# A one-element load moved from the scalar queue into the sync queue, behind the first large load

**Chip, cores, metric.** One NeuronCore of a Trainium2 chip. The metric is the device time of one execution, in microseconds (us).

## The reference

```python
def reference(x, fx, alpha):        # x, fx: bf16 [512, 32, 640]; alpha: bf16 [1]
    return x + alpha * fx
```

x, fx and the result are 20.97 MB each, so 62.92 MB have to move, and VectorE does one multiply-add per element.

## The kernel before

Over 128 partitions each tensor is 128 x 81920, cut into five units of U = 16384 columns (4.19 MB). Every large transfer is issued by the sync engine, in program order. The only other transfer is alpha's one element, issued by the scalar engine (ACT); TensorE spreads it over 128 lanes by a matmul with ones, and VectorE copies it out of PSUM as `a_f`, which all six multiply-adds read.

```python
def alpha_to_lanes(nc, consts, psum, alpha, eng):
    a_1 = consts.tile([1, 1], alpha.dtype, name="a_1")
    eng.dma_start(out=a_1[:], in_=alpha[None, :])
    ones = ...                                      # memset to 1.0 on VectorE
    nc.tensor.matmul(a_ps[:], ones[:], a_1[:], start=True, stop=True)
    nc.vector.tensor_copy(out=a_f[:], in_=a_ps[:])
    return a_f
# ... (cut)
    a_f = alpha_to_lanes(nc, consts, psum, alpha, nc.scalar)
    t_0 = wide.tile([P, 2 * U], x.dtype, tag="a", name="t_0")
    nc.sync.dma_start(out=t_0[:, :U], in_=xv[:, :U])       # x
    nc.sync.dma_start(out=t_0[:, U:], in_=fxv[:, :U])      # fx
# ... (cut)
    x_12 = load_pair("b", 1)                               # 8.4 MB
    f_1 = load_f(1)
    add(t_0[:, :U], t_0[:, U:])
    store(0, t_0[:, :U])
    f_2 = load_f(2)
# ... (cut: x_34 into t_0's buffer, f_3, f_4, the other adds and stores)
```

Of the kernel before, what the change touches and what calls it, by code (L numbers as in the profile page):

```python
# [1 line left out]

# [4 lines left out]

ACT = mybir.ActivationFunctionType
ALU = mybir.AluOpType
F32 = mybir.dt.float32  # L10
BF16 = mybir.dt.bfloat16

U = 16384


def alpha_to_lanes(nc, consts, psum, alpha, eng):

    P = nc.NUM_PARTITIONS
    a_1 = consts.tile([1, 1], alpha.dtype, name="a_1")
    eng.dma_start(out=a_1[:], in_=alpha[None, :])  # L20
    ones = consts.tile([1, P], alpha.dtype, name="ones")
    nc.vector.memset(ones[:], 1.0)  # L22
    a_ps = psum.tile([P, 1], F32, name="a_ps")
    nc.tensor.matmul(a_ps[:], ones[:], a_1[:], start=True, stop=True)  # L24
    a_f = consts.tile([P, 1], F32, name="a_f")
    nc.vector.tensor_copy(out=a_f[:], in_=a_ps[:])  # L26
    return a_f


@with_exitstack  # L30
def kernel(
    ctx: ExitStack,
    tc: tile.TileContext,
    x: bass.AP,
    fx: bass.AP,
    alpha: bass.AP,
    out: bass.AP,
):
    nc = tc.nc
    P = nc.NUM_PARTITIONS  # L40
    xv = x.flatten_outer_dims().rearrange("(p n) d -> p (n d)", p=P)
    fxv = fx.flatten_outer_dims().rearrange("(p n) d -> p (n d)", p=P)
    ov = out.flatten_outer_dims().rearrange("(p n) d -> p (n d)", p=P)
    F = xv.shape[1]
    assert F == 5 * U

    consts = ctx.enter_context(tc.tile_pool(name="consts", bufs=1))
    psum = ctx.enter_context(tc.tile_pool(name="psum", bufs=1, space=bass.MemoryType.PSUM))
    wide = ctx.enter_context(tc.tile_pool(name="wide", bufs=1))
    fs = ctx.enter_context(tc.tile_pool(name="fs", bufs=2))  # L50
    ctx.enter_context(tc.manual_schedule())

    a_f = alpha_to_lanes(nc, consts, psum, alpha, nc.scalar)



    t_0 = wide.tile([P, 2 * U], x.dtype, tag="a", name="t_0")
    nc.sync.dma_start(out=t_0[:, :U], in_=xv[:, :U])  # L58
    nc.sync.dma_start(out=t_0[:, U:], in_=fxv[:, :U])

    def load_pair(tag, u):
        t = wide.tile([P, 2 * U], x.dtype, tag=tag, name="x_t")
        nc.sync.dma_start(out=t[:], in_=xv[:, u * U : (u + 2) * U])
        return t

    def load_f(u):
        t = fs.tile([P, U], fx.dtype, tag="f", name="f_t")
        nc.sync.dma_start(out=t[:], in_=fxv[:, u * U : (u + 1) * U])
        return t

    def add(x_ap, f_ap):
        nc.vector.scalar_tensor_tensor(  # L72
            out=x_ap, in0=f_ap, scalar=a_f[:], in1=x_ap, op0=ALU.mult, op1=ALU.add
        )

    def store(lo, x_ap):
        nc.sync.dma_start(out=ov[:, lo : lo + x_ap.shape[1]], in_=x_ap)

    x_12 = load_pair("b", 1)
# [4 lines that stand above are left out]
    add(x_12[:, :U], f_1[:])  # L84
    x_34 = load_pair("a", 3)
    f_3 = load_f(3)
    add(x_12[:, U:], f_2[:])
    f_4 = load_f(4)
    store(U, x_12[:])
    add(x_34[:, :U], f_3[:])  # L90
    store(3 * U, x_34[:, :U])
    H = U // 2
    for j in range(2):
        add(x_34[:, U + j * H : U + (j + 1) * H], f_4[:, bass.ts(j, H)])
        store(4 * U + j * H, x_34[:, U + j * H : U + (j + 1) * H])


# [1 line left out]
_INS = ['x', 'fx', 'alpha']  # L99
_OUTS = [((512, 32, 640), 'bfloat16')]  # L100


# [23 lines left out]
```

## Time and profile before

| | before |
|---|---|
| time, median of 3 | 152.6 us (152.52 to 152.8) |
| span in the profile | 150.9 us |
| VectorE busy | 86.8 us (58%) |
| packets of the sync queue | 97.8% of sixteen engines' span |
| a_f ready / first add starts | 2.27 / 22.88 us |

The lines, and what they say of the bound, are in the prediction below.

Some words first. An engine *issues* a transfer when it puts it into its queue; the sixteen DMA engines then move it as *packets*, here one for each of 128 rows and, on each engine used, a small one at the end, the *count*, which reports on a semaphore that this engine's share has arrived. A transfer has *landed* when its last count has. The packets that a queue has waiting on one DMA engine are its *ring* there. "Packet records" and "records of landings" are the single packets and semaphore counts of the packed trace, finer than the views shown here.

### The profile page before, as it was taken

The page shows a single profiled execution, that of the slowest core. Times are in us where ns is not written, and L with a number is a line of the kernel's source. Part 1 is how long each engine was busy: PE and PEld are TensorE (multiplying, and loading weights), DVE is VectorE, ACT ScalarE, POOL GpSimd, SP SyncE. Part 2 cuts the span into 40 slices and gives each one's busy share as a digit, 9 for nine tenths or more (in the row PEclk, how much of TensorE's full clock was granted, in tenths as well). Part 3 has the DMA queues.
Part 4 walks back from the last instruction along what each step waited for, and adds up shares of the span by engine and source line. Part 5 has one row for each costly group of instructions (what it writes and reads, how often), then busy time and mean ns, then how long its engine had stood idle before and what let it go on. Part 6 is the DMA issues. An engine that isn't in the chain of part 4 may idle for free.

```text
span 150.9 us, 78 instructions
## 1 busy us (share of the span) xinstructions
PE 0.2 (0%) x1; PEld 0.1 (0%) x1; DVE 86.8 (58%) x8; POOL 0.2 (0%) x4
## 2 busy tenths in 40 slices
PE   0000000000000000000000000000000000000000
PEld 0000000000000000000000000000000000000000
DVE  0000009999600089996799980009999999991000
POOL 0000000000000000000000000000000000000000
DMA  6999996999999899999896969999996969898994
GB/s 226 417 452 426 426 556 278 556 434 400 400 426 426 278 417 417 434 478 512 382 538 295 556 278 426 478 434 426 434 565 295 556 278 556 365 426 373 447 434 178
DMA packets 1874, 62.92 MB, mean 417 GB/s; under 512 B 210, under 2 KB 210, under 8 KB 210
## 3 DMA queue, kind: packets, MB, share of 16 engines
q1 hardware_dynamic: 1872, 62.92, 97.8%
q10 hardware_dynamic: 2, 0.00, 0.0%
HBM read 41.94 MB, written 20.97 MB: 417 GB/s over the span
## 4 chain that ended last, share of the span: by engine, by line
DVE 40%; DMA 35%; another core or an unknown queue 9%; DVEq 6%; SPq 0%; issue 0%
DVE x_t L72 29%; DMA f_t<-in_fx_dram 21%; DMA t<-in_fx_dram 14%; DVE t L72 11%; DVEq L121 6%; SPq L58 0%; DVEq L72 0%
## 5 line engine op out<-in xcount | busy, mean ns | idle before, releaser
L72 DVE SCALAR_TENSOR_TENSOR x_t<-f_t,a_f,x_t 128x16384 bf16<-128x16384 bf16 (+1 forms) x5 | 69.2, 13868 | 26.9 <-DMA f_t<-in_fx_dram 26.9
L72 DVE SCALAR_TENSOR_TENSOR t<-t,a_f 128x16384 bf16<-128x16384 bf16 x1 | 17.3, 17284 | 20.6 <-DMA t<-in_fx_dram 20.6
L26 DVE COPY a_f<-a_ps 128x1 f32<-128x1 f32 x1 | 0.2, 157 | 1.1 <-PE a_ps L24 1.1
L22 DVE MEMSET ones<- 1x128 bf16 x1 | 0.2, 165 | 0.8 <-PEq L110 0.8
L24 PE MATMUL a_ps<-a,ones 1*128 1x1 bf16 x1 | 0.2, 159 | 1.9 <-DMA a<-in_alpha_dram 1.9
L110 POOL MEMSET const-bfloat16-1.0<- 128x1 bf16 x1 | 0.1, 102 | 0.0
L110 POOL MEMSET const-uint8-127<- 128x1 uint8 x1 | 0.1, 102 | 0.0
L24 PEld LDWEIGHTS <-ones 1*128 1x128 bf16 x1 | 0.1, 101 | 1.0 <-DVE ones L22 1.0
L110 POOL MEMSET const-float32-0.0<- 128x1 f32 x1 | 0.1, 99 | 0.2 <-issue 0.2
L110 POOL MEMSET const-float32-1.0<- 128x1 f32 x1 | 0.1, 99 | 0.0
## 6 DMA issues: line engine op xcount, KB each, us to landing
f_t<-in_fx_dram SPq DMA_DIRECT2D x4, 4096.0 KB, 31.9
t<-in_x_dram SPq DMA_DIRECT2D x1, 4096.0 KB, 12.3
t<-in_fx_dram SPq DMA_DIRECT2D x1, 4096.0 KB, 21.6
out_dram<-t SPq DMA_DIRECT2D x1, 4096.0 KB, 22.7
out_dram<-x_t SPq DMA_DIRECT2D x1, 4096.0 KB, 21.3
out_dram<-x_t SPq DMA_DIRECT2D x2, 2048.0 KB, 15.6
x_t<-in_x_dram SPq DMA_DIRECT2D x2, 34.7
a<-in_alpha_dram ACTq DMA_DIRECT2D x1, 0.0 KB
```

Of the source, the lines that this page charges most:

```text
L22: nc.vector.memset(ones[:], 1.0)
L24: nc.tensor.matmul(a_ps[:], ones[:], a_1[:], start=True, stop=True)
L26: nc.vector.tensor_copy(out=a_f[:], in_=a_ps[:])
L72: nc.vector.scalar_tensor_tensor(out=x_ap, in0=f_ap, scalar=a_f[:], in1=x_ap, op0=ALU.mult, op1=ALU.add)
L110: nc = _bacc.Bacc("TRN2", target_bir_lowering=False, num_devices=1)
L121: with _tile.TileContext(nc) as tc:
```

## The change

Its intent: have one issuing engine for all transfers. The element goes into the sync engine's queue behind the first x load, since nobody needs it until the first fx load has landed too.

```diff
-    a_f = alpha_to_lanes(nc, consts, psum, alpha, nc.scalar)
     t_0 = wide.tile([P, 2 * U], x.dtype, tag="a", name="t_0")
     nc.sync.dma_start(out=t_0[:, :U], in_=xv[:, :U])
+    a_f = alpha_to_lanes(nc, consts, psum, alpha, nc.sync)
     nc.sync.dma_start(out=t_0[:, U:], in_=fxv[:, :U])
```

## The prediction

> **What bounds the kernel now.** I read the page first for what is busy, then the sizes and landings of the transfers, then the start of the timeline, then the waits, and the chain of waits last. The page says that nothing but the DMA is near full:
>
> ```profile
> span 150.9 us, 78 instructions
> PE 0.2 (0%) x1; PEld 0.1 (0%) x1; DVE 86.8 (58%) x8; POOL 0.2 (0%) x4
> DMA  6999996999999899999896969999996969898994
> DMA packets 1874, 62.92 MB, mean 417 GB/s; under 512 B 210, under 2 KB 210, under 8 KB 210
> q1 hardware_dynamic: 1872, 62.92, 97.8%
> q10 hardware_dynamic: 2, 0.00, 0.0%
> ```
>
> VectorE works for 58% of the span. The DMA engines are busy in every slice, and the packets of the sync queue, q1, fill 97.8% of sixteen engines' span. The scattered 6s I read as bookkeeping, not gaps: in the page's GB/s row the slices at 278 or 295 stand beside ones at 556 or 565, over the mean, as if rows that cross a slice's edge were counted in the next. Only the first and the last slice, 226 and 178 GB/s, have no such neighbour. The scalar queue, q10, carried two packets: the one element of alpha and the count that reports it.
>
> How fast the engines can go follows from two landings (columns: issues, KB each, us from issue to landing):
>
> ```profile
> t<-in_x_dram SPq DMA_DIRECT2D x1, 4096.0 KB, 12.3
> t<-in_fx_dram SPq DMA_DIRECT2D x1, 4096.0 KB, 21.6
> ```
>
> With issue times 0.73 and 1.17 us from the timeline below, they landed at 13.0 and 22.8 us, 9.7 us apart for 4.194 MB. That is 432 GB/s. All 62.92 MB at this rate take 145.6 us. The span of 150.9 leaves 5.3 us for the way to the first packet, the slow first packets, the last landing and the drain. So this is a transfer floor with little above it, and a change moves the time only if it moves the first packet, makes an engine run out of queued packets, or adds work to the engines.
>
> The start, which is all the change touches (start, duration, engine, line, operation; in brackets the idle time before it and what ended it):
>
> ```profile
> 0.73 0.49 ACTq L20 DMA_DIRECT2D a<-in_alpha_dram  x1
> 0.73 0.38 SPq L58 DMA_DIRECT2D t<-in_x_dram  x1
> 1.17 0.43 SPq L59 DMA_DIRECT2D t<-in_fx_dram  x1
> 1.64 0.42 SPq L63 DMA_DIRECT2D x_t<-in_x_dram  x1
> 1.91 0.16 PE L24 MATMUL a_ps<-a,ones 1*128 1x1 bf16 x1 [1.91 <-DMA a<-in_alpha_dram]
> 2.11 0.52 SPq L68 DMA_DIRECT2D f_t<-in_fx_dram  x1
> 2.11 0.16 DVE L26 COPY a_f<-a_ps 128x1 f32<-128x1 f32 x1 [1.13 <-PE a_ps L24]
> 22.88 17.28 DVE L72 SCALAR_TENSOR_TENSOR t<-t,a_f 128x16384 bf16<-128x16384 bf16 x1 [20.61 <-DMA t<-in_fx_dram]
> ```
>
> The 128-lane alpha, a_f, is ready at 2.11 + 0.16 = 2.27 us, and its first user starts at 22.88, held by the first fx load. Alpha has 20.6 us to spare. The sync engine has issued its four loads by 2.63 us, and then (waits of the sync queue: us in total, times, longest):
>
> ```profile
> SPq L77 <- DVE t L72: 37.5, 1, 37.5
> ```
>
> it stands for 37.5 us until the first add is done. Two loads at the rate above are on chip when that add begins, and 12.6 MB more are queued behind them.
>
> The chain of waits puts 40% on VectorE. I don't take this as the bound: the chain follows semaphores and can't see that while an add holds it, the rings behind are full.
>
> **What the Trainium skill says.** (1) "DMA: Bandwidth & Descriptors", section "Issuing engines are not separate DMA queues": transfers started by different engines run on the same 16 DMA engines and interleave; several issuers save only the sequencer's issue time. The trace agrees on the size of that: 0.49 us on the scalar queue, 0.38 to 0.52 on the sync queue. (2) The same page, "Why a DMA increments its semaphore by 16 and not by 1": a [1,1] transfer from this kind of queue uses one engine, and a 128-partition one all sixteen. The packet counts agree: 2 on q10 (data and count), and on q1 13 transfers x (128 rows + 16 counts) = 1872. (3) The same page, "Queues, rings and completion order": on one engine, descriptors of a ring are consumed in ring order. No run here yet has a small transfer behind a large one; the change is that test. (4) "Perfetto Trace Analysis", section "Roofline": a lone core may exceed its memory share and is held by its 16 DMA engines, about 435 GB/s in total. The measured 432 agrees.
>
> **The change part by part.**
> Removed: the scalar queue's issue, 0.49 us from 0.73. It ran beside the sync engine's own issue and ended nothing on the path: 0.
> Added to the sync engine: one issue between x and fx. I take the alpha issue's own 0.49 us, plus the 0.05 us between issues (0.73 + 0.38 = 1.11, next at 1.17): fx is issued at about 1.17 + 0.54 = 1.7 us, the pair of x at 2.2, f_1 at 2.65. The engines have x to work on until about 12.3 us (the trace's records of landings show the 16 engines finishing x from 12.3 to 13.06). Slack 10.6 us, used 0.54: 0. The sync engine's next wait shrinks from 37.5 to about 37.0: it absorbs the half microsecond.
> Moved: alpha's landing. On its engine it stands behind 8 rows of x (128 rows over 16 engines), so it lands when that engine is through with x: 12.3 to 13.1 us instead of before 1.91. The matmul then starts at about 12.7, and from its start to the end of the copy took 2.27 - 1.91 = 0.36 us: a_f is ready at 12.7 to 13.5. The first add can't start before 22.8. Slack falls from 20.6 to between 9.4 and 10.2 us; cost 0.
> Engine work: the same two tiny packets, on the sync ring instead of the scalar one. The packet records give them 7 and 9 ns. A turn-around gap around them is possible, but the 16 counts at the end of each load are such packets too and leave none: 8 rows of 32 KB with a recorded median of 1.213 us make 9.70 us, which is just the distance of the two landings. I put 0.00 to 0.05 us on one engine.
> First packet: x stays the sync engine's first issue, at 0.73: 0.
> Sum: 0.0 to +0.05 us, against a scatter of the runs before of 0.28 us (152.52 to 152.8).
>
> **Rivals.**
> Alpha becomes the wait: if it were not served in ring order but after all four queued loads, it would land near 53 us (f_1's add began at 53.2). The first add would end near 71, with the engines dry from 53 on: about +17 us, 170. Ring order is against it; even a landing 9 us later than I say would still cost nothing. 1% or less.
> The issue delay carries through: all later loads 0.54 us late gives 153.1. Against it: the engines are backlogged at every one of those issues, and the 37.5 us wait absorbs the delay. 5%.
> A gap on alpha's engine: a 2-byte read from memory takes, issue to matmul, 1.91 - 0.73 = 1.2 us. If the ring stood still for all of it, every load that waits for its slowest engine is up to 1.2 us later: 153.8, still under 1%. Against: the counts leave no gap, and the engines finish a load 0.75 us apart, so part of a gap on an early engine is hidden. 7%.
> A faster start: with the scalar queue silent at 0.73, x's rows may start sooner. They start about 1.0 us after the issue, and alpha's packets went out just before them; I could see 0.1 to 0.2 us, 152.4. 10%.
>
> **Range and chances.** No term reaches 1%, and the only rival that passes 2% needs alpha over 9 us late. The middle is the time before, 152.6. For the range I take the scatter of about 0.3 us either way and stretch it a little upward for the gap and the issue delay: 152.2 to 153.1. Faster by over 2% would have to come from under 149.5 us, and there is no such slack in a span with a 145.6 us floor and an unchanged start: 0.01. Slower: 0.01. Same: 0.98.
>
> **What would show it right or wrong.** The profile after should have no q10 and 1874 packets on q1; an alpha issue of 0.4 to 0.5 us on the sync engine near 1.16 and fx's issue near 1.7; the matmul waiting for alpha until 12.3 to 13.1 us; VectorE's wait split in two, some 12 us for the matmul and 9 to 10 us for fx; the first add still at 22.9 within 0.2; the share of the sync queue within half a point of 97.8%. I am wrong if the first add starts with the copy of a_f, if a slice after the first shows a gap that a neighbour doesn't make up, or if x lands more than half a microsecond away from 13.0.

## The result, and the profile after

| | before | after |
|---|---|---|
| time, median of 6 | 152.69 us (152.38 to 152.89) | 152.5 us (152.36 to 152.73) |
| ratio, 95% interval | | 0.9992 (0.9977 to 1.0006) |
| span in the profile | 150.9 us | 150.7 us |

A ratio here is the mean time of one kernel's fast runs over that of the other's of the same rounds, so not quite the ratio of the medians quoted. This one is the same time: the interval holds 1. (The line numbers of the changed kernel are one or two lower than before.)

The page of the changed kernel: span, the DMA row of the 40 slices, and the only data queue that is left (packets, MB, share of 16 engines).

```profile
span 150.7 us, 78 instructions
...
DMA  6999996979899899999896969999996969798994
...
q1 hardware_dynamic: 1874, 62.92, 97.9%
```

q10 is gone, and its two packets are now on q1. The share is 97.9% where it was 97.8%.

The start of the changed kernel's timeline:

```profile
0.73 0.38 SPq L56 DMA_DIRECT2D t<-in_x_dram  x1
...
1.17 0.32 SPq L20 DMA_DIRECT2D a<-in_alpha_dram  x1
1.54 0.35 SPq L58 DMA_DIRECT2D t<-in_fx_dram  x1
1.94 0.54 SPq L62 DMA_DIRECT2D x_t<-in_x_dram  x1
2.52 0.51 SPq L67 DMA_DIRECT2D f_t<-in_fx_dram  x1
12.91 0.16 PE L24 MATMUL a_ps<-a,ones 1*128 1x1 bf16 x1 [12.91 <-DMA a<-in_alpha_dram]
13.11 0.16 DVE L26 COPY a_f<-a_ps 128x1 f32<-128x1 f32 x1 [12.13 <-PE a_ps L24]
22.70 17.29 DVE L71 SCALAR_TENSOR_TENSOR t<-t,a_f 128x16384 bf16<-128x16384 bf16 x1 [9.43 <-DMA t<-in_fx_dram]
```

All later issues slid by 0.3 to 0.4 us, alpha came 11 us later (matmul at 12.91 instead of 1.91), and the first add still starts when fx lands: 22.70 where it was 22.88. VectorE's one wait of 20.6 us has become two, 12.1 and 9.4. The sync engine paid for its extra issue out of the long wait that follows (waits of the sync queue):

```profile
SPq L76 <- DVE t L71: 37.0, 1, 37.0
```

37.0 us instead of 37.5, the predicted half microsecond; but only 0.4 of it is the extra issue (the last load's issue ends at 3.03 us instead of 2.63). The rest is chance: the first add ended 0.18 us earlier.

One view misleads here. The chain of waits of the changed kernel now lists alpha's issue (start, us, what):

```profile
1.17 0.32 SPq L20
1.49 0.06 issue
1.54 21.03 DMA t<-in_fx_dram
```

It looks like 0.38 us more on the path. The next piece shows otherwise: the fx transfer is counted from its issue, and it took 21.03 us, where the chain of the kernel before has 21.59 for it. A transfer that queues behind 10 us of others here didn't land later for being issued later.

### The profile page after: what moved, and what is told of

Read it like the earlier page. It is cut to its first block, busy times and chain, and to the rows that moved or that the text cites. A ratio compares the mean times of both kernels' runs of the same rounds, so it can differ in the third digit from the quotient of the medians.

```text
span 150.7 us, 78 instructions
## 1 busy us (share of the span) xinstructions
PE 0.2 (0%) x1; PEld 0.1 (0%) x1; DVE 86.8 (58%) x8; POOL 0.2 (0%) x4
## 3 DMA queue, kind: packets, MB, share of 16 engines
q1 hardware_dynamic: 1874, 62.92, 97.9%
## 4 chain that ended last, share of the span: by engine, by line
DVE 40%; DMA 35%; another core or an unknown queue 8%; DVEq 6%; SPq 0%; issue 0%
DVE x_t L71 29%; DMA f_t<-in_fx_dram 21%; DMA t<-in_fx_dram 14%; DVE t L71 11%; DVEq L120 6%; SPq L56 0%; SPq L20 0%; DVEq L71 0%
## 5 line engine op out<-in xcount | busy, mean ns | idle before, releaser
L26 DVE COPY a_f<-a_ps 128x1 f32<-128x1 f32 x1 | 0.2, 157 | 12.1 <-PE a_ps L24 12.1
## 6 DMA issues: line engine op xcount, KB each, us to landing
out_dram<-t SPq DMA_DIRECT2D x1, 4096.0 KB, 22.7
```

## The experiments

The theory under test is the prediction's: the sixteen engines set the time; alpha is hidden by its slack; the issue is hidden by the backlog; the two packets cost nothing. "Before" is always the kernel before, in the same rounds on the same chip.

**again_before and again_after: how much is scatter.** No edit; each kernel once more, with five rounds. They ask whether the 0.08% of the first result, and the tighter landing of x in the first profile after, mean that a silent scalar queue helps.

> The kernel before against itself, for the scatter. Theory (transfer floor) and every rival alike: ratio 1.000, within 0.2%. Read for one thing: whether the 16 engines' spread at the landing of the first x load (0.75 us before, 0.47 us after) comes again at about 0.75. If it comes anywhere from 0.4 to 0.8, the difference between the two first profiles is scatter.

> The changed kernel once more with 5 rounds. Theory (alpha's slack and the backlog hide everything): ratio 0.998 to 1.002. Rival 'a silent scalar queue starts x sooner': ratio 0.998 or below with an interval under 1, x landing at 12.9 with a spread below 0.55 us again.

Measured: again_before 152.48 us, ratio 1.0001 (0.9989 to 1.0013); again_after 152.71 us, ratio 1.0010 (0.9997 to 1.0023). So the changed kernel was 0.08% below in one set of rounds and 0.10% above in the other. In the trace's records of landings the sixteen engines finished x within 0.75 and 0.67 us in the two profiles of the kernel before, within 0.47 and 0.58 us in the two of the changed one, and within 0.92 us in no_alpha below, in which the scalar queue is silent as well. The first row of x began at 1.74 and 1.72 us in the two profiles of the kernel before, at 1.75 and 1.73 in those of the changed one: no earlier. The rival "a faster start" is not borne out; the spread varies from run to run by more than it was to explain.

**alpha_first: the switch of queue alone.** Alpha on the sync queue, but ahead of x.

```diff
+    a_f = alpha_to_lanes(nc, consts, psum, alpha, nc.sync)
     t_0 = wide.tile([P, 2 * U], x.dtype, tag="a", name="t_0")
     nc.sync.dma_start(out=t_0[:, :U], in_=xv[:, :U])
-    a_f = alpha_to_lanes(nc, consts, psum, alpha, nc.sync)
```

> Alpha first on the sync queue, ahead of x: the switch of queue alone, without the place behind x. Theory: here the issue stands ahead of the first packet and nothing hides it, so every landing is later by that issue, 0.38 us (0.32 us and the 0.06 us to the next issue in the profile after): 152.9 to 153.1, ratio 1.0025, x issued near 1.1 and the first fx landing near 23.0. Rival 'the sync engine's issue time never matters': 152.6, ratio 1.000.

Measured: 152.92 us, ratio 1.0032 (1.0018 to 1.0046), about 0.5 us slower, the interval clear of 1. From its timeline:

```profile
0.73 0.33 SPq L20 DMA_DIRECT2D a<-in_alpha_dram  x1
...
1.11 0.35 SPq L57 DMA_DIRECT2D t<-in_x_dram  x1
...
23.28 17.28 DVE L71 SCALAR_TENSOR_TENSOR t<-t,a_f 128x16384 bf16<-128x16384 bf16 x1 [20.98 <-DMA t<-in_fx_dram]
```

x is issued 0.38 us later, by the packet records its first row begins 0.34 us later (2.08 instead of 1.74), and the first add starts 0.40 us later than in the kernel before (22.88; in the nine profiles in which x is issued first and alpha comes no later than fx, tiny_257 apart, it starts between 22.70 and 23.03). The same issue that costs nothing behind x costs about its full length ahead of x (0.3 to 0.7 us by the interval), because only there are the engines empty while it runs. The size rests on the six times: the profiled run is the fastest of them, 152.66 us, and in it f_1 lands at 53.1 us, no later than in the kernel before. The place made the change free; the switch of queue alone would not have been.

**no_alpha: the whole worth of the load.** Nothing is loaded, VectorE writes 1.0 into the 128 lanes. Its output is wrong, which doesn't matter for the time.

```diff
-    a_f = alpha_to_lanes(nc, consts, psum, alpha, nc.sync)
+    a_f = consts.tile([P, 1], F32, name="a_f")
+    nc.vector.memset(a_f[:], 1.0)
```

> No load of alpha at all: the 128 lanes are set to 1.0 by VectorE (a wrong result on purpose). Theory: loading alpha costs nothing on either queue, so 152.4 to 152.7, ratio 0.998 to 1.001, the same as again_after within 0.15%. Rival 'the tiny transfer leaves a gap on its engine' or 'the issue delay carries through': 0.3 to 0.5 us faster than again_after.

Measured: 152.59 us, ratio 1.0008 (0.9997 to 1.0020), beside 1.0010 for again_after in the same rounds. Not loading alpha at all gains nothing that can be seen: the two means differ by 0.07 us, and by their scatter (95%) a gain of more than about 0.35 us is excluded. This disposes of "the delay carries through" at the size that the prediction gave it, 0.5 us.

**behind_fx, behind_x12, behind_f1: how late may alpha be.** The helper's call moves one, two and three places further back in the sync queue, for instance:

```diff
-    a_f = alpha_to_lanes(nc, consts, psum, alpha, nc.sync)
     nc.sync.dma_start(out=t_0[:, U:], in_=fxv[:, :U])
...
     x_12 = load_pair("b", 1)
+    a_f = alpha_to_lanes(nc, consts, psum, alpha, nc.sync)
     f_1 = load_f(1)
```

> Alpha one place further back, behind the first fx load. Theory: it lands with fx near 22.7, the first add starts near 23.1 instead of 22.7 and ends near 40.4, 12 us before the queued loads run out (52.8): 152.5, ratio 1.000. Rival 'once alpha is later than fx its lateness costs one for one': +0.4 us, ratio 1.0025.

> Alpha behind the 8 MB load of the x pair. Theory: it lands near 42.0, the first add runs from 42.4 to 59.7, the queued loads run out at 52.8, and the first store's packets come about 1.1 us after its issue at 59.7: some 8 us without packets, 160 to 161, ratio 1.05. Rival 'one for one beyond fx': +19.7 us, 172. Rival 'the element passes the large loads': 152.5.

> Alpha behind all four loads: the case that the prediction gave 170 us. Theory: it lands near 52.8, the first add runs from 53.2 to 70.5, packets start again near 71.7: 19 us without packets, 171 to 172, ratio 1.125. Rival 'one for one beyond fx': +30.5 us, 183. Rival 'the element passes the large loads': 152.5.

| alpha behind | matmul starts | first add ends | time, us | ratio (95%) |
|---|---|---|---|---|
| x (the change) | 12.91 | 39.99 | 152.5 | 0.9992 (0.9977 to 1.0006) |
| fx | 22.48 | 40.16 | 152.5 | 0.9998 (0.9983 to 1.0012) |
| the x pair | 41.73 | 59.4 | 162.42 | 1.0656 (1.0642 to 1.067) |
| f_1 | 51.41 | 69.1 | 172.2 | 1.1294 (1.1277 to 1.1311) |

The DMA row of behind_x12 and its share:

```profile
DMA  7999999969996009999999699999998998999895
...
q1 hardware_dynamic: 1874, 62.92, 92.2%
```

Two slices are truly empty (0 GB/s in both, which the one slice of 522 GB/s beside them can't make up), and the sync queue's share falls from 97.8% to 92.2%. This is what a gap looks like, unlike the lone 6s. In behind_f1 the matmul and the first store are 17.7 us apart, and the engines have nothing to do:

```profile
51.41 0.16 PE L24 MATMUL a_ps<-a,ones 1*128 1x1 bf16 x1 [51.41 <-DMA a<-in_alpha_dram]
...
69.11 0.37 SPq L75 DMA_DIRECT2D out_dram<-t  x1
...
q1 hardware_dynamic: 1874, 62.92, 86.9%
```

Two things follow. Alpha does stand in ring order: each place back delays the matmul by the transfer it stands behind (9.6, 19.3, 9.7 us). And being later than fx is not enough to cost time: behind_fx takes away the slack to the add and pays nothing, since the add's lateness is hidden by the loads still queued. From the x pair to f_1 the matmul is 9.68 us later and the time 9.78 us longer: only there is lateness paid in full.

The expected size was missed for behind_x12, 160 to 161 against 162.4, and by a little for behind_f1 (171 to 172 against 172.2). The shares tell where the time went. In the kernel before, 97.8% of 150.9 us is 147.6 us of packets on an engine and 3.3 idle; in behind_x12 it is 148.0 and 12.5, in behind_f1 148.2 and 22.3. So the engines idled 9.2 and 19.0 us longer, where I had reckoned with 8 and 19, and the same bytes took about half a microsecond more. I had let the queued loads run out at 52.8 us, when f_1 landed in the changed kernel. But by the packet records nothing moved from 51.27 to 60.28 us in behind_x12 and from 51.25 to 69.97 in behind_f1: f_1 landed at 51.7 us in both, 1.1 us earlier than I had reckoned. In behind_x12 this lengthens the gap; in behind_f1 alpha, which stands behind f_1, comes earlier too, and the gap only moves.

In the profiles of before and after, the packet records show rows from 48 to 51 us that took 1.4 to 2.2 us each instead of 1.21. In the two kernels with a gap those rows were not slow, and slow ones came later (from 69 to 71 and 117 to 119 us in behind_x12, from 78 to 81 and 126 to 129 in behind_f1). When f_1's last rows ran, a store was queued behind f_1 in the former and none in the latter. What slows the rows I have not tested, and it stays open.

**split_pair and in_pair: where the cost begins.** The load of the x pair is cut in two of 4 MB; in in_pair alpha stands between them, in split_pair (the control) behind x as in the changed kernel.

```diff
-    x_12 = load_pair("b", 1)
+    x_12 = wide.tile([P, 2 * U], x.dtype, tag="b", name="x_t")
+    nc.sync.dma_start(out=x_12[:, :U], in_=xv[:, U : 2 * U])
+    a_f = alpha_to_lanes(nc, consts, psum, alpha, nc.sync)      # in_pair alone
+    nc.sync.dma_start(out=x_12[:, U:], in_=xv[:, 2 * U : 3 * U])
```

> The changed kernel with the 8 MB load of the x pair split in two of 4 MB; the control for in_pair. Theory: the engines have queued packets throughout: 152.3 to 152.9, ratio 0.998 to 1.003.

> As split_pair, with alpha between the two halves. In behind_x12 and behind_f1 the time grew by what the first add's end lay past about 49.4 us (59.4 gave +10.0, 69.1 gave +19.7). Theory: alpha lands near 32.2, the first add ends near 49.9, so about half a microsecond of empty engines: 152.7 to 153.4, ratio 1.001 to 1.006, although alpha is 9.5 us later than fx. Rival 'one for one beyond fx': +9.5 us, 162, ratio 1.06.

Measured: split_pair 152.43 us, ratio 1.0004 (0.9984 to 1.0024); in_pair 152.5 us, ratio 1.0029 (0.9986 to 1.0072). The wide interval comes from one of the four runs, 153.72; the others are 152.44, 152.49 and 152.5. The median is under my 152.7 to 153.4, so the half microsecond of empty engines did not come; with that one run in it, the timing can't exclude it. Stretches of the two kernels, first behind_x12, then in_pair (stretch, length, busy time of PE, PEld, DVE and POOL, clock, DMA share, GB/s):

```profile
52.00:60.00 8.00, 0.00 (x0) 0.00 (x0) 8.00 (x2) 0.00 (x0) 1.00 0.00 0
```

```profile
52.00:60.00 8.00, 0.00 (x0) 0.00 (x0) 7.97 (x1) 0.00 (x0) 1.00 1.10 451
```

```profile
31.98 0.16 PE L24 MATMUL a_ps<-a,ones 1*128 1x1 bf16 x1 [31.98 <-DMA a<-in_alpha_dram]
...
49.68 0.35 SPq L75 DMA_DIRECT2D out_dram<-t  x1
...
q1 hardware_dynamic: 2018, 62.92, 98.0%
```

In in_pair the first add ended and the first store was issued at 49.7 us, and nothing stood still: the queue's share is 98.0% (the split load has 144 packets more). So the matmul may start as late as 31.98 us, 9.2 us after fx has landed (22.79), at no cost that the profile shows; at 41.73 it costs 10 us. Rival "one for one beyond fx" (162) falls.

**six_alphas: the suspected costs times six.** Five more one-element loads into spare tiles behind alpha's.

```diff
     a_f = alpha_to_lanes(nc, consts, psum, alpha, nc.sync)
+    for i in range(5):
+        spare = consts.tile([1, 1], alpha.dtype, name=f"spare_{i}")
+        nc.sync.dma_start(out=spare[:], in_=alpha[None, :])
```

> Five more one-element loads behind alpha's, ahead of fx. Theory: six issues of 0.38 us put fx's issue at about 3.4, still 9 us before the engines are through with x, and twelve tiny packets of 7 to 9 ns cost one engine 0.1 us: 152.5 to 152.7, ratio 1.000. Rival 'the issue delay carries through': +1.9 us beyond after, 154.4, ratio 1.012. Rival 'a turn-around gap of 1.2 us for each': up to +6 us, 158.

Measured: 152.68 us, ratio 1.0013 (0.9999 to 1.0028).

```profile
1.52 1.51 SPq L60 DMA_DIRECT2D spare<-in_alpha_dram  x5
3.07 0.36 SPq L61 DMA_DIRECT2D t<-in_fx_dram  x1
12.87 0.16 PE L24 MATMUL a_ps<-a,ones 1*128 1x1 bf16 x1 [12.87 <-DMA a<-in_alpha_dram]
12.93 0.35 SPq L65 DMA_DIRECT2D x_t<-in_x_dram  x1
```

fx is issued 1.5 us later than in the changed kernel. The x pair is issued even 11 us later, which I had not foreseen: its issue waited until x had landed (the waits of the sync queue have 9.5 us for x there). I read that as the ninth transfer reusing the first one's semaphore, since the trace's records give the two the same one. Still no time is lost, because at 12.93 fx fills the engines until 22.7. The rivals' 154.4 and 158 are far off.

**scalar_twice: is it the ring, or just a busy engine?** The kernel before, with the element loaded twice into one tile, so that the second load is issued while x is under way.

```diff
     eng.dma_start(out=a_1[:], in_=alpha[None, :])
+    eng.dma_start(out=a_1[:], in_=alpha[None, :])
```

> The kernel before, with alpha loaded twice into the same tile on the scalar queue; the second load waits for the first and so is issued near 2 us, when x's rows already fill the engines. It tells apart why the element was late in the changed kernel. Theory (it waits for its place in the sync queue's own ring): on the other queue it takes its turn after the row under way, so the matmul starts between 3 and 6 us, not at 12.9. Rival (a busy engine alone delays it): 11 us or later. Time by both: 152.4 to 152.8, ratio 1.000.

Measured: 152.49 us, ratio 1.0003 (0.9988 to 1.0018).

```profile
1.90 0.21 ACTq L21 DMA_DIRECT2D a<-in_alpha_dram  x1
...
7.82 0.16 PE L25 MATMUL a_ps<-a,ones 1*128 1x1 bf16 x1 [7.82 <-DMA a<-in_alpha_dram]
```

The matmul came at 7.82, outside both marks: the theory's range of 3 to 6 is missed, and so is the rival's 11. It overtook x's later rows, which no element in the sync queue did (12.74 to 12.91 in all runs with alpha behind x), so the place in the ring does matter. But it did not take its turn after one row: the packet records have its data 4.5 us after x's first row began, behind three of the eight rows on its engine, and its count 1.2 us later, behind one 32 KB row more. On busy engines the way from issue to matmul took 5.9 us (1.90 to 7.82), where idle ones took 1.2: some lateness comes from the busy engine, and the other 5 us of the changed kernel from the place in the ring. Why it waited for three rows and not for one is open.

**tiny_257: what one tiny packet costs.** Behind alpha, a load of 257 single elements on one engine.

```diff
     a_f = alpha_to_lanes(nc, consts, psum, alpha, nc.sync)
+    many = consts.tile([1, 257], alpha.dtype, name="many")
+    # every second element of a row of fx, 257 separate elements
+    nc.sync.dma_start(out=many[:] ..., in_=fxv[0:1, : 2 * 257] ...[:, :, 0:1])
```

> Behind alpha, one more load of 257 single elements (2 bytes each, every second element of a row of fx, so as many packets on one engine). Theory: such a packet costs its engine what the trace records, 7 to 9 ns, 1.8 to 2.3 us in all, of which up to 0.9 us lies in the spread of the engines: +1 to +2.3 us, 153.4 to 154.8. Rival 'a turn-around of 1.2 us each': +308 us, 460. If it comes out between, the cost of one tiny packet is (time minus 152.5) / 257, and at 50 ns, say, it would be 165; one or two such packets would still be under a tenth of a microsecond.

Measured: 155.7 us, ratio 1.0216 (1.0201 to 1.0231), 3.2 us slower: 1 to 2 us more than expected.

```profile
1.52 0.70 SPq L59 DMA_DIRECT2D many<-in_fx_dram  x1
2.26 11.03 SPq L60 DMA_DIRECT2D t<-in_fx_dram  x1
```

The packets themselves did what I said: in the packet records they start 6 ns apart, 1.5 us for all, from 12.36 to 13.88 us. What I had not expected is fx's issue: the sync engine was held in it for 11.03 us, until 13.29, when some 157 of the 257 elements had started. fx's rows begin at 13.9 to 14.6 us instead of 12.1 to 12.5, on average 1.8 us later. The engines had run dry, and the first row on each took 1.89 us on average instead of 1.21, as x's first rows had at the start (1.93 in the changed kernel). The first add starts 3.1 us later (25.79). The 1.5 us of the tiny packets lie in the stretch in which the other engines stood idle, so they don't come on top: by the trace it is the held issue that costs. What holds it is not tested; it goes with the tiny load ahead of it, of which only this one size was run. For alpha the run means some 6 ns for its data on one engine, and no turn-around.

## Why the prediction was right

The timing alone could not tell: its interval reaches from 0.35 us faster to 0.09 us slower, so it can't separate the sum of 0.00 to 0.05 us from some other small one. What bears the prediction out is the profile, term by term.

- **The bound.** A transfer floor: the share stayed at 97.9%, and of all twelve experiments only those lost clear time that left engines empty (behind_x12, behind_f1, tiny_257) or started them later (alpha_first).
- **The removed issue, 0.** A gain from the silent scalar queue was looked for in three sets of runs (the changed kernel twice, no_alpha) and not found.
- **The added issue, 0.** Shown: 0.38 us is paid ahead of x, not behind it; and behind x not even six of them are paid. Its size was off: I took the scalar engine's 0.49 us, and on the sync engine it took 0.32, so fx was issued at 1.54 and not near 1.7. These two signs on the prediction's list missed; the others came true.
- **Alpha's landing, 12.3 to 13.1.** x's landing ended at 12.88; matmul at 12.91, 0.2 us after the predicted 12.7; a_f ready at 13.27, within 12.7 to 13.5; a slack of 9.43 us where 9.4 to 10.2 was said.
- **The two packets, 0.00 to 0.05 us.** In the changed kernel's own packet records, fx's first row starts 17 ns after the count of x on alpha's engine and 5 to 6 ns after it on the others: the two packets held it up by some 12 ns. Six loads were without cost too.
- **The rival of 170 us** was a true danger, only not of this edit: behind_f1 measured 172.2. The engines idled 19.0 us longer there, where the prediction had put 17, though its own 53 and 71 are 18 apart. It left out the way from the store's issue to its first packet, 0.86 us (69.11 to 69.97).
- **What the prediction didn't say** is that the slack to the first add is not the last line of defence. Another 9 us lie behind it, in the loads that are still queued (in_pair). So "the only rival that passes 2% needs alpha over 9 us late" was too narrow: in in_pair the matmul came 19 us later than in the changed kernel, at no cost.

None of the versions tried beats the two kernels by more than scatter. The change is a matter of tidiness: one queue fewer, at the same time.

## What to carry to other kernels

When the DMA engines are the bound, as here, a small load may stand anywhere in the queue behind the first large one, as long as its user, and then the store that its user releases, comes before the queued loads run out; put ahead of the first large load it costs its issue. Count two slacks, the one to the consumer's other operand and the one to the moment when the queue is empty, and don't take an issue that the chain of waits lists for a cost before you have seen whether the transfer behind it landed later. Beware of a load of many single elements in the same queue: the one tried here held up the next issue for 11 us and cost 3.2 us, with 1.5 us of packets on one engine.

## What the Trainium skill lacked or had wrong

- "DMA: Bandwidth & Descriptors", "Queues, rings and completion order", says that an engine takes turns between queues at packet granularity, a packet being 9 to 17 descriptors as a rule, but not how long a newcomer waits behind rows already under way: in scalar_twice a 2-byte load on an otherwise empty queue moved 4.5 us after the first 32 KB row had begun, behind three of the eight rows, and its count came another 1.2 us later, behind one row; between these two a turn was one row.
- The same page gives no number for when many small descriptors hold up the next issue: behind 257 single elements on one engine, the issue of the next large load took 11.03 us instead of 0.35.
- The same page's fixed cost of about 2 us for a transfer and its figure of about 10.5 ns for a packet are for loads issued from GpSimd; it has none for a tiny load inside a full queue. There a single element's data cost its engine 6 ns (tiny_257), and five further one-element loads cost no measurable time (six_alphas, 1.0013 with an interval that holds 1).
- The same page, "Issuing engines are not separate DMA queues", calls the saved issue time usually small beside the transfer. That holds (0.38 us beside the 9.7 us of a load); what it lacks is where it counts: behind the first load it cost nothing that could be seen (no_alpha 1.0008 beside again_after 1.0010), ahead of it about its length (alpha_first, 1.0032).
